# GpSimd jobs one step later, and a running account of GpSimd's load, in an attention and MoE kernel

## The chip, the cores and the metric

The kernel runs on one core of a Trainium2 chip, in one launch. The metric is the device time of that launch in microseconds (us), as a median over several runs. The engines are TensorE (PE, with its weight loads PEld), VectorE (DVE), ScalarE (ACT), GpSimd (POOL) and SyncE (SP). Each works through its own instructions in the order of the program and waits for others by semaphores.

## The reference

Attention over B = 8 batches, H = 8 heads, S = 576 positions, D = 64, in float32, where each row keeps its 32 highest scores; then a mixture of experts with one expert of eight per token. Cut to what matters:

```python
scores = scale * np.matmul(q, k.transpose(0, 1, 3, 2))      # 8 x 8 x 576 x 576
kth = np.partition(scores, -32, axis=-1)[..., -32:-31]
attn = softmax of the scores that are >= kth                # the others are masked
x = matmul(attn, v), transposed to (8 * 576, 512)           # 4608 tokens
logits = x @ w_gate                                         # 8 experts
expert, gate_w = argmax(logits), its softmax probability
out[token] = gate_w * (relu(x @ w1[expert]) @ w2[expert])   # 512 -> 1024 -> 512
```

## The kernel before, in words

**The attention loop.** A loop over steps t takes 16 half batches n of NT = 9 steps s each, 144 steps in all. A step handles two tiles of 128 rows. PE computes their scores three steps ahead and ACT copies them to SBUF (tile sb). VectorE finds the 32nd highest score of each row: 21 MAX8 over parts of sb into cand (L1025), then rounds of MAX8 and MATCH_REPLACE8 on cand that fill vq (L1033). GpSimd makes the bound nb from vq (L1007), ACT the sign of sb against nb (sg, L454), and GpSimd adds sg to sb in two instructions (L455), "the pair". This pair marks what is masked. PE then transposes sb (tt, L461), ACT takes exponentials, and PE multiplies by the values (px, L477 and L492).

**Side jobs.** Everything else is cut into generators, each in one of the lanes prep0, prep1, sums, rows, redo, patch, find, route. Once a step, `advance` goes through the lanes by due time and lets each run to its next `yield`. A `need(...)` states what the next piece takes of each engine; a piece whose need would bring what was spent in this step above `LIMITS` waits for a later step, as does one whose s is not among its `at`. `need(slack=1)` is a pause of a step without a price; after the loop, where no limits hold, it is skipped. What a piece does on PE, ACT, VectorE and GpSimd goes to queues that are flushed at fixed places of the step; VectorE's pieces are interleaved with the rounds of the search. The scatters of `route` and the DMAs on SP's queue are emitted at once.

The jobs that matter here, once for each batch b:

- sums: ACT writes exponentials of the kept values over vq, GpSimd adds them up (vq 128x288 down to 128x18, and tiny), VectorE takes the reciprocal (rinv). apart, cnt and wild on GpSimd count what was kept.
- find: rows for which the search may have kept a wrong number are looked for and up to 128 of them are picked: r_key, r_ok, r_sl, r_qx on VectorE, a product with r_qx on PE (r_li), then r_fl on VectorE, and gathers by r_fl of r_at and r_nb and by r_at of the scores r_sb, on GpSimd.
- redo: does these rows again: r_wk and r_v on VectorE, then a subtraction r_sb by r_wk on GpSimd, exponentials r_et, the product of rv and r_et on PE (L265), and r_xa. patch writes them over the first result (scatters lps, xs). Their pieces may run at the steps s in FREE, FREE2 and FREE3 only.
- rows: normalises the output (xm, lp, xl, lpl on VectorE) and stores it as tokens xs.
- route: gate logits lg, expert choice oh, hist and cum on VectorE, positions po and pos, the payload pay, and five scatters into `table` on GpSimd, each with a spacer ahead (L846 and L847). Batch 4 fixes the rows of the first expert, batch 5 those of four more (`ahead`): for these two all five scatters go out in one piece, followed by hist x ones on PE, skip and ebase on VectorE and the loads of the indices ids.

top, a running maximum over the half batches, is updated by GpSimd at the last step of each.

**The MoE part.** After the loop the remaining jobs are drained, first on their own until the first expert is routed, then piece by piece with the steps of the generator `moe`. It goes through units (an expert and up to some tiles of 128 tokens); each has eight steps f over F = 1024. A step is a hidden product H (ph, L1159), and the projection of the step before (y, L1174). Its weights are split in a high and a low part: wh on ACT or VectorE, wl on VectorE for w1 and on GpSimd for w2 (L957). Unit 0's weights are split ahead, into the tiles rv and kt. Rows of a unit are gathered by GpSimd (kt for unit 0 and gx later, L876), turned by PE (mt and ph from kt or gx, L1139) and split by ACT (xh) and VectorE (xl). From f = 3 on, the tiles of the next unit are turned one a step, if they have been gathered by then; if not, all are turned together ahead of that unit's first step. A unit's rows can be gathered only when route has run for the batch that fixes them.

L265 is the line of a helper that flushes the queues, so most jobs stand under it.

Of the kernel before, what the change touches and what calls it, by code (L numbers as in the profile page):

```python
# [14 lines left out]
OP = mybir.AluOpType  # L15
# [22 lines left out]
CAP = 640  # L38
TAIL = 1
TADV = 5  # L40
FREE = (1, 2, 3, 4, 5)
FREE2 = (1, 2, 3, 4)
FREE3 = (1, 2, 3)
DUE = dict(redo=4, patch=12, sums=0, rows=0, find=3, route=12)
LIMITS = dict(pool=3.5, act=1.6, dve=2.0, pe=3.0)


@with_exitstack
def attention_moe(ctx, tc, q, k, v, w_gate, w1, w2, out):
    nc = tc.nc  # L50
# [37 lines left out]
    NT = 2 * MAIN + 1  # L88
# [98 lines left out]
    top = consts.tile([128, 1], F32, name="top")  # L187
# [76 lines left out]
    def later(queue):  # L264
        return lambda f, *a, **k: queue.append(lambda: f(*a, **k))  # L265

    pe, act, vec, pool = later(pq), later(aq), later(dq), later(gq)
# [8 lines left out]
    def need(**k):  # L276
        return k
# [157 lines left out]
    MX = {}  # L435
# [178 lines left out]
    def j_find(b):  # L614
# [39 lines left out]
        yield need(dve=0.1)  # L654
        fl = sm("r_fl", [128, 1], I32)
        vec(nc.vector.scalar_tensor_tensor, fl, li[:, 1:2], float(NLT + 1), li[:, 0:1], op0=OP.mult, op1=OP.add)
        yield need(pool=2.0)
        at = sm("r_at", [128, 4], I32)
        pool(nc.gpsimd.indirect_dma_start, out=at, out_offset=None, in_=atab,
# [129 lines left out]
    def j_route(b):  # L789
# [49 lines left out]
        vec(nc.vector.tensor_reduce, sm, ex, axis=AX.X, op=OP.add)  # L839
        vec(nc.vector.tensor_scalar, sm, sm, 1e-9, None, op0=OP.add)  # L840
        vec(nc.vector.reciprocal, pay[:, :, 2].bitcast(F32), sm)
        for c in range(KB):
            if c == 0 or b not in ahead:
                yield need(pool=1.0)
            n = 128 if c < MAIN else LEFT
            nc.gpsimd.memset(spacer, 0.0)  # L846
            st = nc.gpsimd.indirect_dma_start(  # L847
                out=table, out_offset=bass.IndirectOffsetOnAxis(ap=pos[0:n, c:c + 1], axis=0),
                in_=pay[0:n, c, :], in_offset=None)
            for o in scat:  # L850
                tc.declare_no_dep(st.ins, o.ins, reason="each token has a slot of its own")
            scat.append(st)
# [30 lines left out]
    ROUTED = set()  # L883
    lanes = {k: [] for k in ("prep0", "prep1", "sums", "rows", "redo", "patch", "find", "route")}
    wants = {}

    def start(lane, job, due=0):
        lanes[lane].append((due, job))
# [1 line left out]
            wants[lane] = next(job)  # L890

    def advance(limits=LIMITS, s=None):
        spent = {}
        for name in sorted((k for k in lanes if lanes[k]), key=lambda k: lanes[k][0][0]):
            lane, want = lanes[name], wants[name] or {}
            want = dict(want)
            if s not in want.pop("at", (s,)) and s is not None:
                continue
            want["bank"] = want.get("bank", 0) + want.pop("spot", 0)
            if not att_open[0]:  # L900
                want["bank"] += want.pop("nook", 0)
            if want.get("bank", 0) > len(free) or want.get("nook", 0) > cell[0]:
                continue
            if limits and any(spent.get(r) and spent[r] + want[r] > limits[r] for r in want if r in limits):
                continue
            for r in want:
                spent[r] = spent.get(r, 0.0) + want[r]
            cell[0] -= want.get("nook", 0)
            wants[name] = next(lane[0][1], lanes)
            while not limits and wants[name] and wants[name] is not lanes and wants[name].get("slack"):  # L910
                wants[name] = next(lane[0][1], lanes)
            if wants[name] is lanes:
                wants[name] = None
                lane.pop(0)
                if lane:
                    wants[name] = next(lane[0][1])

    def drain(more=None):
        while any(lanes.values()):
# [84 lines left out]
    for t in range(steps + LAG + TD + 4):  # L1004
        n, s = divmod(t, NT)
        if delayed:
            delayed[0](*delayed[1])  # L1007
        if grp(t - LAG - TD - 1):
            exps(t - LAG - TD - 1)
        if grp(t - LAG):  # L1010
            softmax(t - LAG, grp(t - LAG), 0)
        scores(grp(t + LA))
        if grp(t - LAG):
            softmax(t - LAG, grp(t - LAG), 1)
        if grp(t - LAG - TD - 2):
            av(t - LAG - TD - 2, grp(t - LAG - TD - 2))
        scores_left(grp(t + LA))
        if grp(t - LAG - TD):
            transp(t - LAG - TD)
        flush(pq)  # L1020
        flush(aq)
        one, two, last = topk(t, grp(t)) if grp(t) else ([], [], None)
        for m in range(max(len(one), 1)):
            if m < len(one):
                one[m][0](*one[m][1])  # L1025
        delayed = last
        if t == 1:
            settle(first_pt, [0, 1, 2, 3], lambda: release(first_pt))
            mine_, dq[:] = dq[:], []
            flush(mine_)  # L1030
        mine, dq[:] = dq[:], []
        for m, (f, a) in enumerate(two):
            f(*a)  # L1033
            if mine and m >= 2:
                mine.pop(0)()
        flush(mine)
        if t == 0:
            nc.vector.tensor_reduce(top, VQ[0][:, 0:2, 0], axis=AX.X, op=OP.max)
            first_pt = bank()
            spread(first_pt)  # L1040
            pq.pop()()
        if s == NT - 1 and n in MX:
            pool(nc.gpsimd.tensor_scalar, top, MX.pop(n), top, None, op0=OP.max)
        m = t - LAG + 1
        if m > 0 and m % (2 * NT) == 0:
            start("find", j_find(m // (2 * NT) - 1), t + DUE['find'])
            start("redo", j_redo(m // (2 * NT) - 1), t + DUE['redo'])
        m = t - LAG
        if 0 <= m < steps and m % NT == NT - 1:
            start("sums", j_sums(m // NT), t + DUE['sums'])  # L1050
            if m == steps - 1 and len(lanes["sums"]) == 1:

                for _ in range(2):
                    wants["sums"] = next(lanes["sums"][0][1])
                flush(gq)
                flush(aq)
        if t < steps:
            advance(s=s)
            flush(gq)
        else:  # L1060
            for _ in range(TAIL if t < steps + TADV else 0):
                advance(None)
                for queue in (gq, pq, aq, dq):
                    flush(queue)
        for at, job, a in AHEAD if first else ():
            if t - steps == at:
                job(*a)
        m = t - LAG - TD - 3
        if m >= 0 and m % NT == NT - 1:
            start("rows", j_rows(m // NT), t + DUE['rows'])  # L1070
        if s == PA:
            prep(2 * n + 4)
        if s == PB:
            prep(2 * n + 3)
        if s == LQ and n + 2 < NQ:
            load_qk(n + 2)
        if s == LV and 0 < n < NQ:
            load_v(n)
# [367 lines left out]
    n = over(moe_a, counts, cap, otab, lambda: next(g))  # L1446
# [50 lines left out]
```

## Time and profile before

| | |
|---|---|
| runs | 1308.88, 1307.54, 1308.72 us; median 1308.72 |
| profiled execution | 1306.47 us, its span 1304.6 us, granted clock 0.984 |
| busy, share of the span | PE 1217.7 us (93%), PEld 968.0 (74%), DVE 1019.4 (78%), ACT 828.3 (63%), POOL 833.6 (64%) |
| chain of waits, share | DVE 51%, PE 36%, POOL 4%, issue 4%, DMA 2%, ACT 2%, SP's queue 1% |

The attention loop ends with VectorE's last search at 762.4 us. The first matmul of the MoE part (mt from kt) starts at 787.97 us. The chain lies on VectorE in the loop and on PE in the MoE part; the shares over the whole span mix the two. A row of the timeline gives start and duration in us, engine, line, operation, and in brackets the engine's idle time before it with what ended it.

### The profile page before, as it was taken

What the parts mean: (1) busy time and instruction counts of PE and PEld (TensorE: products, weight loads), DVE (VectorE), ACT (ScalarE), POOL (GpSimd) and SP (SyncE); (2) the same over time, 40 slices, a digit from 0 to 9 for tenths busy, and PEclk for the clock granted to TensorE, in tenths of its full rate; (3) what the DMA queues carried; (4) which work ended last, traced back from release to release, by engine and by line L of the source; (5) the groups of instructions that cost most, each with busy time, mean ns of one, the idle gap of its engine ahead of it and who ended that gap; (6) DMA issues with size and microseconds to landing.
All of it is one profiled execution on the core that took longest, in us unless ns stands there. A gap on an engine that the chain in (4) does not pass through costs nothing.

```text
span 1304.6 us, 31672 instructions
## 1 busy us (share of the span) xinstructions
PE 1217.7 (93%) x9126; PEld 968.0 (74%) x9126; DVE 1019.4 (78%) x6889; ACT 828.3 (63%) x1691; POOL 833.6 (64%) x1205
## 2 busy tenths in 40 slices
PE   6999999999999999999998878999899999999997
PEld 3667666776666666667676667888899989889996
DVE  7998999999999999999998965645773333345664
ACT  4999789898888888887996843333332323233432
POOL 4676766877867867868867866675554324155654
PEclk9999999999999999999998988999999999999999
DMA  6755565655655655555553615645564434256774
GB/s 168 228 176 180 174 188 157 185 172 159 190 164 156 194 178 170 167 173 168 182 174 110 191 39 163 189 118 170 138 184 139 121 99 127 79 157 191 223 212 125
DMA packets 271239, 211.18 MB, mean 162 GB/s; under 512 B 136216, under 2 KB 214216, under 8 KB 271056
## 3 DMA queue, kind: packets, MB, share of 16 engines
q1 hardware_dynamic: 260320, 185.92, 48.2%
q0 software_dynamic: 9504, 22.86, 5.4%
q8 instruction: 74, 1.21, 0.4%
q14 instruction: 109, 0.89, 0.2%
q10 hardware_dynamic: 1232, 0.30, 0.1%
HBM read 102.49 MB, written 107.90 MB: 161 GB/s over the span
## 4 chain that ended last, share of the span: by engine, by line
DVE 51%; PE 36%; POOL 4%; issue 4%; DMA 2%; ACT 2%; SPq 1%; POOLq 0%; DVEq 0%; ACTq 0%
DVE cand L1025 25%; PE ph L1159 16%; PE y L1174 16%; DVE cand L1033 10%; DVE vq L1033 9%; PE mt L1139 1%; DVE xm L265 1%; PE pt L265 1%; POOL sb L455 1%; POOL table L847 1%; DMA gx<-xs,ids 1%; DVE r_v L265 1%; DVE r_qx L265 1%; POOL wl L957 1%; SPq L113 1%
## 5 line engine op out<-in xcount | busy, mean ns | idle before, releaser
L455 POOL TENSOR_TENSOR sb<-sb,sg 128x576 f32<-128x576 f32 x288 | 370.0, 1301 | 50.7 <-ACT sg L454 41.1
L1025 DVE MAX8 cand<-sb 128x8 f32<-128x52 f32 (+2 forms) x3024 | 368.5, 208 | 0.2 <-issue 0.2
L957 POOL TENSOR_TENSOR wl<-r,wh 128x512 fp32r<-128x512 f32 x110 | 142.0, 1292 | 223.4 <-DVE wh L956 219.0
L454 ACT ACTIVATE sg<-sb,nb 128x576 int8<-128x576 f32 x288 | 228.9, 795 | 60.8 <-POOL sb L455 60.8
L477 PEld LDWEIGHTS px<-et,rv 128*64 128x64 f32 x2688 | 130.2, 137 | 122.0 <-ACT xt L265 49.0
L1160 ACT ACTIVATE hh<-ph 128x320 fp32r<-128x320 f32 (+3 forms) x136 | 58.2, 428 | 241.2 <-PE ph L1159 214.5
L1033 DVE MAX8 vq<-cand 128x8 f32<-128x22 f32 (+7 forms) x1152 | 200.6, 205 | 0.0
L461 PE MATMUL tt<-turner,sb 128*128 128x128 f32 x1296 | 177.7, 279 | 22.2 <-POOL sb L455 18.7
L367 PE MATMUL ps<-qk 64*128 64x512 f32 (+1 forms) x576 | 185.7, 653 | 4.2 <-ACT sb L369 3.5
L1161 DVE SCALAR_TENSOR_TENSOR hl<-ph,hh 128x320 fp32r<-128x320 f32 (+3 forms) x136 | 65.1, 479 | 150.3 <-ACT hh L1160 124.1
L467 ACT ACTIVATE et<-tt,shift 128x1152 f32<-128x1152 f32 x144 | 178.2, 1237 | 2.5 <-PE tt L461 2.5
L477 PE MATMUL px<-et,rv 128*64 128x128 f32 (+1 forms) x2688 | 163.5, 267 | 13.4 <-ACT xt L265 8.0
L461 PEld LDWEIGHTS tt<-turner,sb 128*128 128x128 f32 x1296 | 147.9, 144 | 34.4 <-POOL sb L455 29.3
L1159 PE MATMUL ph<-xh,wh 128*128 128x320 f32 (+3 forms) x536 | 168.2, 314 | 0.0
L1159 PE MATMUL ph<-xh,wl 128*128 128x320 f32 (+3 forms) x536 | 164.8, 307 | 0.0
L1159 PE MATMUL ph<-xl,wh 128*128 128x320 f32 (+3 forms) x536 | 164.6, 307 | 0.0
L1033 DVE MATCH_REPLACE8 cand<-vq,cand 128x22 f32<-128x22 f32 (+2 forms) x864 | 158.6, 189 | 0.0
L369 ACT ACTIVATE sb<-ps 128x1024 f32<-128x1024 f32 x144 | 149.0, 1034 | 10.3 <-PE ps L367 10.3
L1174 PE MATMUL y<-wh,hl 128*128 128x512 f32 x324 | 128.4, 396 | 0.0
L1174 PE MATMUL y<-wh,hh 128*128 128x512 f32 x324 | 127.7, 394 | 0.5 <-ACT yo L1178 0.5
L1174 PE MATMUL y<-wl,hh 128*128 128x512 f32 x324 | 127.9, 395 | 0.0
L1159 PEld LDWEIGHTS ph<-xh,wh 128*128 128x128 f32 x536 | 101.0, 188 | 3.9 <-issue 1.0
(261 smaller groups left out, 2174.4 us busy)
## 6 DMA issues: line engine op xcount, KB each, us to landing
r<-in_moe_w_dram SPq DMA_DIRECT2D x220, 256.0 KB
sc<-sb SPq DMA_DIRECT2D x128, 288.0 KB
sc<-sb SPq DMA_DIRECT2D x128, 256.0 KB
rv<-in_v_dram SPq DMA_DIRECT2D x32, 256.0 KB
xs<-xm SPq DMA_DIRECT2D x16, 512.0 KB
rq<-in_q_dram SPq DMA_DIRECT2D x60, 128.0 KB
rk<-in_k_dram SPq DMA_DIRECT2D x60, 128.0 KB
sc<-sb SPq DMA_DIRECT2D x32, 144.0 KB
```

What stands on the lines that cost most here:

```text
L367: nc.tensor.matmul(MAINS[:, n], qk[:, 0, w], qk[:, 1, 2 * LEFT:], start=True, stop=True)
L369: nc.scalar.activation(bass.AP(EX[-1].tensor, EX[-1].offset, [list(EX[-1].ap[0]), [S + LEFT, 2], [1, M]]), MAINS, AF.Copy)
L454: nc.scalar.activation(upper(SG[i]), SB[u], AF.Sign, bias=nb[:, i, 1:2], accum_out=CNT[b][:, 2 * lt + i:2 * lt + i + 1])
L455: nc.gpsimd.tensor_tensor(SB[u], SB[u], SG[i], op=OP.add)
L461: nc.tensor.matmul(tt[:, c], x[:, c * 128:(c + 1) * 128], ident, start=True, stop=True, is_transpose=True)
L467: nc.scalar.activation(ET[t], three.rearrange("p (c q) -> p c q", c=NB9), AF.Exp, bias=shift[:, t // NT, 0:1], scale=0.125)
L477: yield lambda kb=kb, blk=blk: nc.tensor.matmul(px[h * 64:(h + 1) * 64], block(rv, p % 2, kb if kb < MAIN else MAIN + n, h), et[:, blk, q] ...
L957: (nc.gpsimd if i else nc.vector).tensor_tensor(lo, r, hi, op=OP.subtract)
L1025: one[m][0](*one[m][1])
L1033: f(*a)
L1159: nc.tensor.matmul(ph, a[:, c, :], x[:, c, s], start=(m == 0), stop=(m == len(seq) - 1))
L1174: nc.tensor.matmul(PY[u, t], a[:, s], x, start=(f == 0 and m == 0), stop=(f == FC - 1 and m == 2))
```

## The change

Three things change in the order in which jobs are handed out:

- FREE, FREE2, FREE3 move by one step; find pauses a step between r_fl and its gathers, route one between pay and the first scatter; top is updated at the first step of the next half batch instead of the last of its own.
- The pool limit of a step falls from 3.5 to 3.0.
- What a step has spent on GpSimd above ROOM = 2.2 is carried into the next as `debt` and counts there as spent.

```diff
-FREE = (1, 2, 3, 4, 5)
-FREE2 = (1, 2, 3, 4)
-FREE3 = (1, 2, 3)
+FREE = (2, 3, 4, 5, 6)
+FREE2 = (2, 3, 4, 5)
+FREE3 = (2, 3, 4)
-LIMITS = dict(pool=3.5, act=1.6, dve=2.0, pe=3.0)
+ROOM = 2.2
+LIMITS = dict(pool=3.0, act=1.6, dve=2.0, pe=3.0)
...
         vec(nc.vector.scalar_tensor_tensor, fl, li[:, 1:2], float(NLT + 1), li[:, 0:1], op0=OP.mult, op1=OP.add)
+        yield need(slack=1)
         yield need(pool=2.0)
...
         vec(nc.vector.reciprocal, pay[:, :, 2].bitcast(F32), sm)
+        yield need(slack=1)
         for c in range(KB):
...
+    debt = [0.0]
...
     def advance(limits=LIMITS, s=None):
-        spent = {}
+        spent = {"pool": debt[0]} if limits and debt[0] else {}
...
+        if limits:
+            debt[0] = max(spent.get("pool", 0.0) - ROOM, 0.0)
...
-        if s == NT - 1 and n in MX:
-            pool(nc.gpsimd.tensor_scalar, top, MX.pop(n), top, None, op0=OP.max)
+        if s == 0 and n - 1 in MX:
+            pool(nc.gpsimd.tensor_scalar, top, MX.pop(n - 1), top, None, op0=OP.max)
```

Lines of the changed kernel are numbered a little higher: L1007 becomes L1014, L847 L850, L876 L879, L957 L964, L1139 L1146.

In the loop, GpSimd's order around the gathers of batch 2, before. nb and two sb rows are the work of a step; r_at and r_nb are the gathers by r_fl:

```order
L455 TENSOR_TENSOR sb<-sb,sg_145 128x576
L846 MEMSET spacer 1x1
L847 DMA table<-pay,pos 36864x4
L265 TENSOR_SCALAR top<-mx_n,top 128x1
L265 DMA r_at<-atab,r_fl 128x4
L265 DMA r_nb<-ntab_5133,r_fl 128x2
L1007 TENSOR_TENSOR nb_232<-vq,factors 128x4
L455 TENSOR_TENSOR sb<-sb,sg_143 128x576
```

and with the change:

```order
L456 TENSOR_TENSOR sb<-sb,sg_143 128x576
L456 TENSOR_TENSOR sb<-sb,sg_145 128x576
L266 TENSOR_SCALAR top<-mx_n,top 128x1
L266 IOTA pay 128x5
L1014 TENSOR_TENSOR nb_232<-vq,factors 128x4
L456 TENSOR_TENSOR sb<-sb,sg_143 128x576
L456 TENSOR_TENSOR sb<-sb,sg_145 128x576
L266 DMA r_at<-atab,r_fl 128x4
L266 DMA r_nb<-ntab_5098,r_fl 128x2
L266 TENSOR_SCALAR apart<-vq,shift 128x18
L266 TENSOR_TENSOR cnt<-cnt,apart 128x18
L266 TENSOR_SCALAR apart<-vq,shift 128x18
```

top now comes after the pair of the next step and the gathers a step later, together with the counts apart, cnt and wild.

Between the loop and the MoE part, GpSimd's order before, from the second kt gather to the first of the four additions that finish the sums of the last half batch:

```order
L876 DMA kt<-xs,ids_12353 128x512
L846 MEMSET spacer 1x1
L847 DMA table<-pay,pos 36864x4
L846 MEMSET spacer 1x1
L847 DMA table<-pay,pos 36864x4
L846 MEMSET spacer 1x1
L847 DMA table<-pay,pos 36864x4
L846 MEMSET spacer 1x1
L847 DMA table<-pay,pos 36864x4
L846 MEMSET spacer 1x1
L847 DMA table<-pay,pos 36864x4
L265 TENSOR_TENSOR vq<-vq 128x18x8
```

and with the change, from the same gather on:

```order
L879 DMA kt<-xs,ids_13110 128x512
L266 TENSOR_TENSOR vq<-vq 128x18x8
L266 TENSOR_TENSOR vq<-vq 128x18x4
L266 TENSOR_TENSOR vq<-vq 128x18x2
L266 TENSOR_TENSOR vq<-vq 128x18
L266 TENSOR_TENSOR vq<-vq,tiny 128x18
L964 TENSOR_TENSOR rv_13422<-rq,rv_13421 128x512
L964 TENSOR_TENSOR kt<-rk,kt 128x512
L266 IOTA pay 128x5
L964 TENSOR_TENSOR wl_13568<-r_13525,wh_13567 128x512
L849 MEMSET spacer 1x1
L850 DMA table<-pay,pos 36864x4
```

The five scatters of batch 5 stood ahead of the sums and now stand behind the first wl of the MoE part.

The gathers of unit 1 on GpSimd before, where wl is the second of the MoE part:

```order
L957 TENSOR_TENSOR wl_13629<-r_13592,wh_13628 128x512
L875 MEMSET spacer 1x1
L876 DMA gx<-xs,ids_13517 128x512
L875 MEMSET spacer 1x1
L876 DMA gx<-xs,ids_13517 128x512
L875 MEMSET spacer 1x1
L876 DMA gx<-xs,ids_13517 128x512
L265 DMA r_at<-atab,r_fl 128x4
```

and with the change, where the last wl ahead of them is the sixth:

```order
L964 TENSOR_TENSOR wl_13760<-r_13704,wh_13759 128x512
L266 TENSOR_TENSOR r_xa<-r_xa 128x256
L266 TENSOR_TENSOR r_xa<-r_xa 128x128
L266 TENSOR_TENSOR r_xa<-r_xa 128x64
L964 TENSOR_TENSOR wl_13819<-r_13754,wh_13818 128x512
L878 MEMSET spacer 1x1
L879 DMA gx<-xs,ids_13784 128x512
L878 MEMSET spacer 1x1
L879 DMA gx<-xs,ids_13784 128x512
L878 MEMSET spacer 1x1
L879 DMA gx<-xs,ids_13784 128x512
```

They come four wl later, behind the scatters and the pieces of find and redo of the last batches. Since they come later, PE's order changes as well. Before, four transposes of gx at a time stood between the steps of unit 0:

```order
L1174 MATMUL y_13638<-wh_13597,hh 128x512
L1174 MATMUL y_13638<-wl_13598,hh 128x512
L1174 MATMUL y_13638<-wh_13597,hl 128x512
L1139 MATMUL mt<-turner,gx 128x128 x4
L265 MATMUL pt_247<-turner,xt 128x144 x2
L265 MATMUL pt_247<-turner,xt 64x144 x2
```

and with the change all twelve stand behind unit 0, ahead of the first hidden product of unit 1 (ph 128x384):

```order
L1181 MATMUL y_13618<-wh_13759,hh 128x512
L1181 MATMUL y_13618<-wl_13760,hh 128x512
L1181 MATMUL y_13618<-wh_13759,hl 128x512
L1146 MATMUL mt<-turner,gx 128x128 x12
L1166 MATMUL ph<-xh,wh_13874 128x384
L1166 MATMUL ph<-xl_13945,wh_13874 128x384
L1166 MATMUL ph<-xh,wl_13875 128x384
```

The rv x r_et products of batch 6, ten matmuls each, move too: both stood ahead of the r_qx product in the gap, now one stands between it and the first mt, and one behind the first projection of unit 0.

## The prediction

> **What bounds the kernel now.** I read the busy time of three stretches first: the attention loop up to VectorE's last top-k search, the gap up to the first MoE matmul, and the MoE part.
>
> ```profile
> 0.00:762.50 762.50, 701.23 (x6135) 505.80 (x6136) 744.30 (x6346) 647.74 (x1329) 552.86 (x875) 0.99 0.57 171
> 762.50:788.00 25.50, 16.57 (x129) 13.16 (x128) 10.87 (x32) 9.01 (x17) 20.49 (x34) 0.80 0.24 61
> 788.00:1304.60 516.60, 499.93 (x2868) 449.05 (x2864) 264.22 (x512) 171.59 (x345) 260.26 (x297) 0.99 0.51 153
> ```
>
> The columns after the length are PE, PEld, DVE, ACT, POOL. VectorE (DVE) is busy 744.30 of 762.50 us in the loop, so an edit is worth there what it takes from VectorE's own queue. In the 25.5 us of the gap POOL leads with 20.49. In the MoE part PE is busy 499.93 of 516.60. Three places, three owners: an edit to GpSimd's order counts where GpSimd makes the owner wait, or where the owner's instruction runs longer beside GpSimd's.
>
> A loop step without side jobs, the last two steps, and the end of the last:
>
> ```profile
> 745.05 1.14 DVE L1025 MAX8 cand<-sb 128x8 f32<-128x52 f32 x9
> 749.63 1.02 DVE L1025 MAX8 cand<-sb 128x8 f32<-128x52 f32 x8
> 756.14 1.02 DVE L1025 MAX8 cand<-sb 128x8 f32<-128x52 f32 x8
> 762.39 0.53 DVE L265 TENSOR_TENSOR xm<-pt,rinv 128x384 f32<-128x384 f32 x1
> ```
>
> Each row is the first search of a step (the last: what follows the final one). The bare step is 749.63 - 745.05 = 4.58; steps 142 and 143 take 6.51 and 6.25, the excess being side jobs interleaved with the search.
>
> **The loop, part by part.** Excess that is not work but waiting shows in three side jobs and one wait:
>
> ```profile
> L265 DVE SCALAR_TENSOR_TENSOR r_fl<-r_li x8: 148/783/1428, 143.8 to 798.3; 128x1 int32<-128x1 f32 x8
> L265 DVE TENSOR_TENSOR r_wk<-sg,r_sb x8: 745/750/1779, 182.4 to 818.1; 128x576 f32<-128x576 bf16 x8
> L265 DVE TENSOR_TENSOR hist<-oh,valid x8: 321/792/1210, 287.8 to 893.1; 128x40 bf16<-128x40 f32 x8
> DVE skip L265 <- PE pt L265: 5.5, 1, 5.5
> 327.64 2.52 POOL L455 TENSOR_TENSOR sb<-sb,sg 128x576 f32<-128x576 f32 x2
> 328.76 1.43 DVE L265 SCALAR_TENSOR_TENSOR r_fl<-r_li 128x1 int32<-128x1 f32 x1
> ```
>
> The last two rows give the mechanism: r_fl has one element per partition, and beside GpSimd's pair of mask additions (327.64 to 330.16) it ends at 330.19, when the pair does. Here POOL was late, so its pair lay over r_fl; where POOL is on time r_fl takes 0.148.
>
> (1) r_fl. Four of the eight are long (the median, 783, is halfway between 148 and some 1,420). The change puts top, r_at and r_nb a step behind what they read; POOL no longer waits for VectorE in its queue ahead of the pair, and r_fl's step has an early pair. -4 x 1.28 = -5.1 us (ends: 0 and -5.1).
> (2) r_wk and hist. Two r_wk (at 182.4 and 369.0) are 1.0 longer than the median, and four hist in the loop take the median, 0.47 over the shortest: -2.0 and -1.9; the new steps of hist have a short queue on POOL. Ends: 0 and -3.9.
> (3) r_wk's new place. It moves from steps 70, 88, ... to 72, 90, 108, 126, right after POOL's heaviest stretch. The prices on POOL:
>
> ```profile
> 326.48 0.98 POOL L847 DMA_INDIRECT table<-pay,pos  x1 [0.16 <-issue]
> 345.73 0.20 POOL L1007 TENSOR_TENSOR nb<-vq,factors 128x4 f32<-128x4 f32 x1
> 345.88 2.52 POOL L455 TENSOR_TENSOR sb<-sb,sg 128x576 f32<-128x576 f32 x2
> 348.79 1.65 POOL L265 TENSOR_TENSOR r_xa<-r_xa 128x256 f32<-128x256 f32 x3
> 357.78 1.53 POOL L265 TENSOR_TENSOR vq<-vq 128x144 f32<-128x144 f32 x4
> ```
>
> nb and the pair are 2.67 a step, an indirect DMA with its spacer 1.26. In the new order POOL has, in the eight steps before r_wk's, 8 x 2.67 = 21.4; nine indirect DMAs = 11.3; r_xa 1.65; sums 1.8; about 4.8 of small operations: 41.0. VectorE's eight steps are 8 x 4.58 and 2.8 of jobs = 39.4. So POOL comes to that step about 1.6 us late, and the pair ends 1.6 us into r_wk, which comes 2.84 into a step. Four times: +6.4 (ends: 0 where POOL is on time, and 4 x 2.5, the whole pair, = +10.0). I take 1.6 because the sum gives it. [...]
>
> (4) Work leaves the loop. The r_wk group of batch 6 (step 142: 6.51 - 4.58 - 0.28 for rinv, as at 784.17 below, = 1.6) and the lg group of batch 5 (step 143: 6.25 - 4.58 - 0.53 for xm = 1.1) come after the last search, where VectorE waits for POOL anyway: -2.7. If that cover were gone, 0.
> (5) The skip wait. Its chain:
>
> ```profile
> 690.27 1.09 POOL L847 DMA_INDIRECT table<-pay,pos  x1 [2.42 <-DVE vq L1033]
> 698.52 2.51 POOL L455 TENSOR_TENSOR sb<-sb,sg 128x576 f32<-128x576 f32 x2
> 709.52 0.16 DVE L265 TENSOR_SCALAR skip<-pt 128x1 f32<-128x1 f32 x1 [5.50 <-PE pt L265]
> ```
>
> Batch 4's five scatters go in one burst; the next pair starts at 698.52, PE's transposes wait for it, hist x ones stands behind them on PE, and skip behind that on VectorE. In the new order the burst still stands in one piece, but without the 2.42, and skip comes four steps after it instead of three. I take 5.5 down to 2.3 (0.3 to 1.9 more recovered by one more step): -3.2, ends 0 and -5.5.
>
> Loop: -5.1 - 3.9 + 6.4 - 2.7 - 3.2 = -8.5.
>
> **The gap before MoE.**
>
> ```profile
> 775.74 0.09 POOL L846 MEMSET spacer<- 1x1 f32 x1
> 782.30 1.53 POOL L265 TENSOR_TENSOR vq<-vq 128x144 f32<-128x144 f32 x4
> 784.17 0.28 DVE L265 RECIPROCAL rinv<-vq 128x8 f32<-128x8 f32 x2 [5.24 <-POOL vq L265]
> 787.72 0.37 PE L265 MATMUL pt<-rhs,r_qx 128*128 128x2 bf16 x8 [4.59 <-DVE r_qx L265]
> 787.97 1.09 PE L1139 MATMUL mt<-turner,kt 128*128 128x128 f32 x4
> 775.29 2.60 PE L265 MATMUL pt<-rv,r_et 128*128 128x256 f32 x10
> ```
>
> Batch 5's five scatters fill POOL from 775.74 to 782.30, and the last sums, rinv, r_qx and the first MoE transposes (mt) wait in a row for that. The change puts these scatters behind the sums: -6.6. The r_sb subtraction now ahead of the sums costs 0.4 (the rest falls in a POOL wait), and the first of the two rv x r_et products, which lay under the scatters, now stands between r_qx and mt: +2.5. Together -3.7; ends -6.2 (the product finds cover) and -1.5 (VectorE is late with batch 5's lg group).
>
> **The MoE part.** The second rv x r_et product moves from the gap to unit 0: +2.5, since PE is full there. The larger term is unit 1's rows:
>
> ```profile
> 786.53 2.03 POOL L265 TENSOR_TENSOR r_xa<-r_xa,r_hm 128x512 f32<-128x512 f32 x1
> 796.19 1.29 POOL L957 TENSOR_TENSOR wl<-r,wh 128x512 fp32r<-128x512 f32 x1 [7.63 <-DVE wh L956]
> 799.92 1.02 POOL L876 DMA_INDIRECT gx<-xs,ids  x1 [0.16 <-issue]
> 802.81 0.95 POOL L876 DMA_INDIRECT gx<-xs,ids  x1 [0.22 <-issue]
> 804.79 0.60 PE L1139 MATMUL mt<-turner,gx 128*128 128x128 f32 x4
> 806.06 0.69 DVE L1141 TENSOR_TENSOR xl<-mt,xh 128x512 fp32r<-128x512 f32 x1 [0.50 <-ACT xh L1140]
> 814.72 2.55 POOL L957 TENSOR_TENSOR wl<-r,wh 128x512 fp32r<-128x512 f32 x2
> 819.55 0.33 PE L1159 MATMUL ph<-xh,wh 128*128 128x384 f32 x1
> 876.31 5.26 DMA gx<-xs,ids
> 791.71 0.63 PE L1159 MATMUL ph<-xh,rv 128*128 128x256 f32 x2
> 794.91 0.49 PE L1159 MATMUL ph<-xh,rv 128*128 128x256 f32 x2
> ```
>
> Times from mt (787.97). Now the gathers go out at +12 and the three tiles are turned between steps of unit 0; unit 1's first matmul is at 819.55, +31.6. In the new order the five scatters follow the first wl on POOL, and the gathers follow the sixth, so that all twelve transposes stand together in front of unit 1. First wl at +8.2; from there to the end of the sixth wl POOL takes 21.1 now, of which 4.1 are gathers and 1.0 a wait; with 6.6 of scatters and 2.0 of r_xa,r_hm it is 24.6. Gathers at +33.0; a gather that PE waited for took 5.26 to its use: first tile +38.3, third 2.6 later, and mt to the end of xl 2.0: unit 1 starts at +42.9, against +34.1 with the product alone. That is +8.8; with 1.0 for r_xa,r_hm (as it runs undisturbed) 7.8: I take +8.3. Ends: +3.7, if rows land with the issue's end, and +9.
>
> After such a pause PE may run slow: after the 4.59 above, two matmuls took 0.63 at 791.71 and not before 794.91 less, half speed for 4.3, some 2.1 lost. I take +1.5, between 0 and 2.1. [...]
>
> MoE: 2.5 + 8.3 + 1.5 = +12.3. Order and waits after unit 1 stay, as PE paces them.
>
> **Sum**: -8.5 - 3.7 + 12.3 = +0.1 on the profiled 1306.47. The median of the runs is 1308.72, 0.2% above it, so 1308.8: no measurable change (0.2%, 2.6 us, is about what can be told).
>
> **Rivals.**
> A, faster: r_wk is not behind the pair, since POOL arrives on time (1.6 us in 41 is small, and jobs of the loop are spread by the account). The +6.4 goes: 1302.4. For it: six of eight r_wk take 0.75 now. Against: the 41.0 against 39.4.
> B, faster: unit 1's rows land early. At the low end (+3.7, clock kept) MoE costs 6.2: 1302.7. For it: the first gather of 799.92 was used at 804.79 without a wait. Against: the third gather's issue alone ends near +37.
> C, slower: POOL falls further behind in unit 0. Its list there is 24.6 us without a hole, and r_xa,r_hm takes 2.03 beside VectorE; every us later starts unit 1 a us later. From 2.5 it decides; at 4, wl is late for PE too: 1313. Against: each wl waits for a cast of VectorE that follows PE, so the list cannot fall behind by much more than its own length.
> D: nothing moves, since VectorE was 98% busy and GpSimd only followed: 1308.7. Against: r_fl, and the 5.5 at skip.
>
> **How the numbers follow.** As summed: 0.42, of which 0.29 falls within 0.2%, 0.06 below and 0.07 above. A 0.21, B 0.10, C 0.22, D 0.05. Faster 0.06 + 0.31 = 0.37, same 0.29 + 0.05 = 0.34, slower 0.07 + 0.22 = 0.29. The range reaches beyond A and C, whose other terms vary by a few us: 1300.5 to 1315.5; my own case alone has 1304 to 1313.
>
> **What the profile will show.** Right: r_fl at 0.15 in all loop steps; r_wk near 2.3 in four; POOL waits for mx_n gone; a skip wait of 1 to 3.5; the gap at 21 to 22.5; a PE wait of 5 to 6 for gx ahead of unit 1. Wrong: r_wk at 0.75 (A), a gx wait of 2 (B) or 9 (C), or PE waiting for wl in unit 0.

## The result, and the profile after

| | before | after |
|---|---|---|
| median of the runs, us | 1308.13 (1305.07 to 1308.88) | 1321.21 (1318.64 to 1322.18) |
| span of the profiled execution, us | 1304.6 | 1316.9 |
| granted clock | 0.984 | 0.978 |

The change makes the kernel slower: the ratio is 1.0102, with a 95% interval of 1.0085 to 1.0119. The forecast was no change, 1308.8 us, with 1315.5 as the upper end. The profiled run of the changed kernel is the fastest of its four, so its stages add up to 12.3 more than before where the medians differ by 13.1.

The same three stretches of the changed kernel (length, then PE, PEld, DVE, ACT, POOL busy; the first value behind them is the granted clock):

```profile
0.00:758.03 758.03, 698.22 (x6125) 505.00 (x6127) 740.84 (x6332) 650.23 (x1325) 547.61 (x874) 0.99 0.59 172
758.03:783.42 25.39, 16.40 (x130) 12.97 (x129) 16.36 (x46) 10.15 (x21) 16.06 (x24) 0.82 0.37 104
783.42:1316.90 533.48, 508.60 (x2875) 455.81 (x2874) 268.05 (x512) 172.16 (x345) 266.18 (x307) 0.97 0.49 146
```

The loop is 4.4 us shorter (758.03 against 762.47), where 8.5 was forecast. The gap is 25.4 as before, where 3.7 less was forecast. The MoE part is 16.8 longer, where 12.3 was forecast. All three miss in the same direction, so that 0.1 became 12.3.

**The loop.** The side jobs of VectorE in the changed kernel (count, then min/median/max in ns), and two of them before:

```profile
L266 DVE SCALAR_TENSOR_TENSOR r_fl<-r_li x8: 144/160/455, 143.5 to 793.8; 128x1 int32<-128x1 f32 x8
L266 DVE TENSOR_TENSOR hist<-oh,valid x8: 316/325/371, 307.6 to 905.8; 128x40 bf16<-128x40 f32 x8
L266 DVE TENSOR_TENSOR r_wk<-sg,r_sb x8: 737/1212/1857, 186.9 to 815.7; 128x576 f32<-128x576 bf16 x8
L266 DVE SCALAR_TENSOR_TENSOR r_key<-cnt,idx x8: 185/742/774, 110.1 to 767.6; 128x36 f32<-128x36 f32 x8
L266 DVE COPY hist<-cum x8: 177/623/1066, 308.4 to 906.7; 128x8 bf16<-128x8 bf16 x8
```

```profile
L265 DVE SCALAR_TENSOR_TENSOR r_key<-cnt,idx x8: 183/186/196, 110.1 to 770.3; 128x36 f32<-128x36 f32 x8
L265 DVE COPY hist<-cum x8: 173/177/561, 289.1 to 894.0; 128x8 bf16<-128x8 bf16 x8
```

r_fl and hist are short everywhere, as forecast. r_wk is long in four steps, by 1.0 each. Two operations that the forecast never looked at are new on the list: r_key rose from 0.19 to 0.74 in five steps, and the copy into hist from 0.18 to 1.06 in four. How they come to wait (GpSimd's pair and VectorE's operation, at three places):

```profile
386.51 2.52 POOL L456 TENSOR_TENSOR sb<-sb,sg 128x576 f32<-128x576 f32 x2
388.32 0.76 DVE L266 SCALAR_TENSOR_TENSOR r_key<-cnt,idx 128x36 f32<-128x36 f32 x1
...
403.29 2.52 POOL L456 TENSOR_TENSOR sb<-sb,sg 128x576 f32<-128x576 f32 x2
403.55 1.07 DVE L266 COPY hist<-cum 128x8 bf16<-128x8 bf16 x1
...
375.08 2.51 POOL L456 TENSOR_TENSOR sb<-sb,sg 128x576 f32<-128x576 f32 x2
376.44 1.78 DVE L266 TENSOR_TENSOR r_wk<-sg,r_sb 128x576 f32<-128x576 bf16 x1
```

An addition of the pair is half of 2.52. r_key starts in the second one and ends with it (389.08 against 389.03). The copy starts in the first and ends with the first (404.62 against 404.55). r_wk starts just behind the first (376.44 against 376.34) and ends 0.63 behind the second (378.22 against 377.59). So each waits for the one addition that runs when it comes. Before, the wait also went the other way: eight of the 288 additions ran long, 1.53 to 2.33, four of them begun while r_wk ran. In the changed kernel none takes over 1.30, so of the two it is VectorE alone that waits there.

**The skip wait** went from 5.5 to 4.5. The burst has moved, but more work stands behind it:

```profile
738.18 0.91 POOL L850 DMA_INDIRECT table<-pay,pos  x1 [0.22 <-issue]
739.11 1.53 POOL L266 TENSOR_TENSOR vq<-vq 128x144 f32<-128x144 f32 x4
743.52 1.66 POOL L266 TENSOR_TENSOR r_xa<-r_xa 128x256 f32<-128x256 f32 x3
751.09 0.16 DVE L266 TENSOR_SCALAR skip<-pt 128x1 f32<-128x1 f32 x1 [4.55 <-PE pt L266]
```

The last scatter is followed by the end of a sum and by r_xa, 3.2 in all, before GpSimd catches up with the pairs that PE needs ahead of hist x ones.

**The gap.** ScalarE, GpSimd and PE between the last search (758.03) and the first MoE matmul:

```profile
761.67 0.78 ACT L266 ACTIVATE r_wk<-r_sb,r_nb 128x576 bf16<-128x576 f32 x1 [4.39 <-DVE r_v L266]
762.35 1.20 ACT L468 ACTIVATE et<-tt,shift 128x1152 f32<-128x1152 f32 x1
764.39 2.51 POOL L456 TENSOR_TENSOR sb<-sb,sg 128x576 f32<-128x576 f32 x2 [3.19 <-ACT sg L455]
777.24 2.25 DVE L266 TENSOR_TENSOR r_qx<-slots,r_sl 128x1024 bf16<-128x1024 bf16 x1
779.76 3.73 PE L266 MATMUL pt<-rv,r_et 128*128 128x256 f32 x10
783.42 1.12 PE L1146 MATMUL mt<-turner,kt 128*128 128x128 f32 x4
```

The redo of batch 6 now comes after the last search. ScalarE's part of it waits 4.39 for r_v and stands in ScalarE's queue ahead of the last exponentials (et) and signs (sg); GpSimd's last pair waits for these, and the sums, r_qx and mt follow it.

**The MoE part**, from GpSimd's first wl to unit 1's first product; the last three rows are of the chain of waits:

```profile
791.75 1.29 POOL L964 TENSOR_TENSOR wl<-r,wh 128x512 fp32r<-128x512 f32 x1 [13.24 <-PE ph L1166]
798.62 0.91 POOL L850 DMA_INDIRECT table<-pay,pos  x1 [0.22 <-issue]
815.64 1.05 POOL L879 DMA_INDIRECT gx<-xs,ids  x1
820.81 0.66 PE L1146 MATMUL mt<-turner,gx 128*128 128x128 f32 x4 [4.14 <-DMA gx<-xs,ids]
822.88 1.11 PE L1146 MATMUL mt<-turner,gx 128*128 128x128 f32 x4 [1.41 <-DVE xl L1148]
825.40 1.12 PE L1146 MATMUL mt<-turner,gx 128*128 128x128 f32 x4 [1.41 <-DVE xl L1148]
827.21 0.69 PE L1166 MATMUL ph<-xh,wh 128*128 128x384 f32 x1 [0.69 <-ACT xh L1147]
828.42 0.52 PE L1166 MATMUL ph<-xh,wl 128*128 128x384 f32 x1
...
815.64 5.12 DMA gx<-xs,ids
885.74 6.86 DMA gx<-xs,ids
893.82 3.62 PE ph L1166 x12
```

Unit 1 starts 43.8 after the first MoE matmul (827.21 - 783.42), against 31.6 before: +12.2. Its first product runs at half clock (0.52 a matmul, where 0.33 is usual) and costs 2.3, of which 1.7 remain from the third step on. The granted clock was 0.50 in it, and 1.00 in that of the kernel before. The gather of unit 3's rows took 6.86 to its use, against 5.26 before: PE waits 4.85 for them (3.48 before), and the product behind this wait starts 1.7 later still. It is slow too, 3.62 for 12 matmuls at a granted clock of 0.55, another 1.6. These are the 16.8 within 0.4.

### The profile page after: what moved, and what is told of

The parts are those of the page before. It is cut to its first block, busy times and chain, and to the rows that moved or that the text cites. A ratio compares the mean times of both kernels' runs of the same rounds, so it can differ in the third digit from the quotient of the medians.

```text
span 1316.9 us, 31664 instructions
## 1 busy us (share of the span) xinstructions
PE 1223.2 (93%) x9126; PEld 973.8 (74%) x9126; DVE 1025.2 (78%) x6889; ACT 832.5 (63%) x1691; POOL 829.9 (63%) x1205
## 4 chain that ended last, share of the span: by engine, by line
PE 43%; DVE 34%; POOL 7%; issue 5%; ACT 5%; DMA 4%; SPq 2%; POOLq 0%; DVEq 0%; ACTq 0%
DVE cand L1032 16%; PE ph L1166 16%; PE y L1181 15%; DVE cand L1040 7%; DVE vq L1040 6%; PE pt L266 3%; POOL sb L456 3%; PE ps L368 2%; PE px L478 2%; PE mt L1146 2%; ACT sg L455 2%; PE tt L462 1%; DMA gx<-xs,ids 1%; ACT sb L370 1%; DMA rv<-in_v_dram 1%
## 5 line engine op out<-in xcount | busy, mean ns | idle before, releaser
L456 POOL TENSOR_TENSOR sb<-sb,sg 128x576 f32<-128x576 f32 x288 | 363.6, 1280 | 42.9 <-ACT sg L455 34.2
L964 POOL TENSOR_TENSOR wl<-r,wh 128x512 fp32r<-128x512 f32 x110 | 142.6, 1297 | 233.5 <-DVE wh L963 216.9
L455 ACT ACTIVATE sg<-sb,nb 128x576 int8<-128x576 f32 x288 | 225.7, 784 | 24.5 <-POOL sb L456 24.2
L478 PEld LDWEIGHTS px<-et,rv 128*64 128x64 f32 x2688 | 132.0, 139 | 118.0 <-ACT xt L266 47.4
L1014 POOL TENSOR_TENSOR nb<-vq,factors 128x4 f32<-128x4 f32 x144 | 29.1, 202 | 142.7 <-DVE vq L1040 108.2
```

What stands on the lines that cost most here:

```text
L455: nc.scalar.activation(upper(SG[i]), SB[u], AF.Sign, bias=nb[:, i, 1:2], accum_out=CNT[b][:, 2 * lt + i:2 * lt + i + 1])
L456: nc.gpsimd.tensor_tensor(SB[u], SB[u], SG[i], op=OP.add)
L478: yield lambda kb=kb, blk=blk: nc.tensor.matmul(px[h * 64:(h + 1) * 64], block(rv, p % 2, kb if kb < MAIN else MAIN + n, h), et[:, blk, q] ...
L964: (nc.gpsimd if i else nc.vector).tensor_tensor(lo, r, hi, op=OP.subtract)
```

## The experiments

All by stage: the ratio to before with its interval, the end of VectorE's last search, the gap from there to the first MoE matmul, from there to unit 1's first matmul, and from that to the end of the last engine instruction, behind which every span goes on for about 6.5 (us, one profile each; two profiles of one order differ by up to 2 in a stage).

| run | ratio | search ends | gap | to unit 1 | rest |
|---|---|---|---|---|---|
| before | | 762.5 | 25.5 | 31.6 | 478.5 |
| after | 1.0102 (1.0085 to 1.0119) | 758.0 | 25.4 | 43.8 | 483.1 |
| e1_free_shift | 0.9982 (0.9971 to 0.9993) | 758.3 | 21.2 | 34.4 | 482.0 |
| e2_no_find_pause_last | 0.9989 (0.9973 to 1.0005) | 760.7 | 24.4 | 30.8 | 482.9 |
| e3_top_and_route_pause | 0.9936 (0.9919 to 0.9953) | 753.4 | 25.4 | 32.4 | 479.6 |
| e4_find_pause_and_shift | 1.0146 (1.0118 to 1.0173) | 770.6 | 24.4 | 38.5 | 485.9 |
| e5_without_find_pause | 0.9961 (0.9945 to 0.9977) | 752.1 | 20.6 | 34.8 | 483.6 |
| e6_exp_first | 1.0079 (1.0062 to 1.0097) | 758.6 | 20.5 | 47.4 | 483.2 |
| e7_turn_in_three_banks | 1.0061 (1.0038 to 1.0084) | 757.4 | 24.3 | 40.2 | 484.0 |
| e8_no_idle_before_unit_1 | 1.0094 (1.0076 to 1.0111) | 758.8 | 24.3 | 43.6 | 483.7 |
| e9_route_sooner | 1.0101 (1.0075 to 1.0127) | 757.0 | 25.9 | 47.0 | 479.1 |
| e10_no_find_pause_route_sooner | 0.9879 (0.9857 to 0.9900) | 749.8 | 20.5 | 39.7 | 471.9 |
| e11_route_pause_alone | 0.9957 (0.9938 to 0.9977) | 754.2 | 25.4 | 32.4 | 479.1 |
| e12_top_alone | 0.9979 (0.9964 to 0.9995) | 759.0 | 25.7 | 31.2 | 480.9 |
| e13_no_idle_at_all | 1.0053 (1.0031 to 1.0074) | 757.5 | 24.3 | 41.8 | 482.0 |
| e14_r_key_and_r_wk_later | 1.0073 (1.0049 to 1.0097) | 755.5 | 26.5 | 45.6 | 484.5 |
| e15_best_with_r_wk_later | 0.9947 (0.9927 to 0.9968) | 759.6 | 21.7 | 43.4 | 471.9 |

### Which part of the change costs

**e1**, before with `FREE`, `FREE2`, `FREE3` shifted alone:

> The kernel before with FREE, FREE2 and FREE3 moved by one step and nothing else of the change. Theory A (a late tail: a shift of one step puts batch 5's route so late that unit 1's rows are gathered after unit 0's sixth wl, and all twelve transposes stand together ahead of unit 1): unit 1 starts with its three tiles turned one after the other, but the scatters already ran in the gap, so the rows have landed; the chain of three tiles costs some 5 us against 1.3 now, and PE runs at half clock behind it (1 to 2): 1312 to 1315. Rival B (the loss comes from GpSimd's work in the loop, by the account and the lower limit): no change, 1308.

A miss: it is a little faster. The order in unit 1 is the one with all twelve transposes together, but here the gathers go out 46 after the last search and not 58, so unit 1 loses only 2.8, and 3.5 later; loop and gap win 8.5.

**e2**, the changed kernel with find's pause for the first six batches only:

```diff
-        yield need(slack=1)
+        if b < 6:
+            yield need(slack=1)
```

> The changed kernel, with find's pause left out for batches 6 and 7 only; the loop up to step 135 is the same as in the changed kernel. In its order unit 1's tiles are turned between the steps of unit 0 again, both rv x r_et products stand ahead of the gap's end, and skip stands four steps after the burst, in step 140. Theory A: the 16.8 us of the MoE part go away, and the gap shrinks by the scatters: 1301 to 1306. Rival B: the loss stays with the loop's order: 1318 to 1322.

The loss at unit 1 is gone (30.8), and with it the whole of the slowdown: batch 5's first scatter goes out 19 after the last search and unit 1's first gather 36, against 35 and 58 in the changed kernel. 4.4 stay in the rest, most of it in waits for later units' rows. The total is at the upper end of A.

**e3**, before with top a step later and route's pause, **e11** with route's pause alone, **e12** with top alone:

> The kernel before with only two parts of the change: top one step later, and route's pause. The tail is that of the kernel before; skip stands in step 136, six steps after the burst instead of three. Theory A: the skip wait (5.5 us) goes, and with POOL no longer waiting for mx_n ahead of a pair, the long r_fl shrink (up to 5 us): 1298 to 1304. Rival C (a wait taken from POOL comes back somewhere else in the loop, since VectorE was busy nearly all the time): 1306 to 1309.

> Before, with route's pause alone. A (its pay no longer keeps GpSimd waiting, and skip comes six steps behind the burst of scatters): the skip wait falls from 5.5 to under 1, r_fl stays long in four steps: 1301 to 1304. B (the pause helps only once GpSimd's waits for the running maximum are gone): skip 3 or more, 1305 to 1308.

> Before, with top a step later alone. A (GpSimd's wait for mx_n in its queue is what makes the pair late where r_fl comes): r_fl 0.15 in all steps, skip still 5.5: 1301 to 1304. B (the waits for pay make it late): r_fl long in four steps, 1306 to 1308.

e3 is as expected, and faster than both kernels. Apart, the two parts do other things than I thought. r_fl in e11, then in e12, and the skip wait in the same order:

```profile
L265 DVE SCALAR_TENSOR_TENSOR r_fl<-r_li x8: 147/150/657, 141.4 to 790.1; 128x1 int32<-128x1 f32 x8
L265 DVE SCALAR_TENSOR_TENSOR r_fl<-r_li x8: 148/439/1421, 143.4 to 795.0; 128x1 int32<-128x1 f32 x8
...
DVE skip L265 <- PE pt L265: 1.1, 2, 0.6
DVE skip L265 <- PE pt L265: 5.5, 2, 5.0
...
POOL table L847 <- DVE vq L1033: 12.0, 5, 2.4
```

Route's pause alone shortens r_fl and the skip wait; with top alone r_fl stays long in four steps and skip waits 5.0. The last row shows GpSimd waiting for VectorE ahead of a scatter, in e12 as before; in e11 these five waits are gone. So what made the pair late for r_fl was a scatter that waited for pay in GpSimd's queue, not the running maximum. hist does the opposite: it stays at 0.8 in e11 and is 0.32 in e12.

**e4**, before with find's pause and the shift of `FREE`:

> The kernel before with find's pause and the FREE shift alone (the pause cannot stand without the shift), without the account, route's pause and top. Theory A: this carries the whole loss of the tail: 1316 to 1322. Rival B: without the account the loss is gone: 1306 to 1310.

Slower than expected: the loop alone loses 8.1. GpSimd is late there because it waits in its queue, and VectorE then waits for it:

```profile
DVE skip L265 <- PE pt L265: 7.5, 1, 7.5
DVE r_key L265 <- POOL cnt L265: 3.1, 3, 1.7
DVE mm L265 <- ACT stat L265: 1.5, 1, 1.5
```

So the other parts of the change (route's pause, top, the account) take back some of what find's pause costs; which of them does it in the loop I did not separate.

**e5**, the changed kernel without find's pause:

```diff
         vec(nc.vector.scalar_tensor_tensor, fl, li[:, 1:2], ...)
-        yield need(slack=1)
         yield need(pool=2.0)
```

> The changed kernel without the pause of find; all other parts are in. A (the pause of find brings r_wk behind the pair, the new waits of r_key and of the copies into hist, and batch 5's late routing): the loop as in the run with top and route alone (-9), the gap as in the run with the shift of FREE alone (-4), the MoE part +3 to +7: 1298 to 1304. B (the account of GpSimd's load spreads jobs so that VectorE's short operations meet the pair): the loop near -3, so 1305 to 1310.

As expected, though the MoE part is 8.3 longer than before and not 3 to 7. It is 1.4% faster than with the pause: the loop wins 5.9, the gap 4.8 and unit 1's start 9.0. In this kernel r_key is 0.19 in the loop steps and the copy into hist 0.17, and batch 5's first scatter goes out 18 after the last search, against 35 with find's pause and 14 before. Adding the pause to the shift of `FREE` costs the like (e1 to e4, 1.6%). This one line is the slowdown. It is not what lengthens r_wk: in the steps of the loop r_wk stands 3.5 over its shortest in all, against 4.0 with the pause, and 3.7 in e3.

### What the three stages lose

**e6**, the changed kernel with ScalarE's r_wk of batch 6 one round later:

```diff
+        if b == B - 2:
+            for _ in range(1):
+                yield
         yield need(act=0.6)
```

> The changed kernel, with ScalarE's r_wk of batch 6 one round later in the drained part, so that the last et and sg stand ahead of it. A (ScalarE's queue held back the last pair of GpSimd and with it the sums and r_qx: 4.39 us at r_wk): the last pair starts at least 2.5 earlier, the gap falls from 25.4 to 21 to 23; one product of r_et moves into the MoE part (+2.5 there): 1317 to 1319.5. B (the gap is set by another chain, GpSimd's own list or the late products): gap 25, 1321 to 1323.

```profile
759.32 4.99 POOL L456 TENSOR_TENSOR sb<-sb,sg 128x576 f32<-128x576 f32 x4
```

The two last pairs now stand back to back, the second from 761.8, 3.2 after the last search and not 6.4, and r_qx comes 2.4 sooner. The gap is 4.9 shorter, 2.4 of it by that and 2.5 because the product with r_et moves behind mt. A holds for the gap. But unit 1 starts 67.9 after the last search, against 69.2: its gathers went out only 1.1 earlier, and 3.6 of the 4.9 come back there. The two ratios, 1.0079 and 1.0102, have intervals that meet, so that the stages show more here than the whole.

**e7**, tiles 2 and 3 of unit 1 turned in the banks of ph:

```diff
-        pt = ps_a.tile([128, DC, 128], F32, name="mt") if u or not t else \
+        pt = ps_a.tile([128, DC, 128], F32, name="mt") if u > 1 or not t else \
```

> The changed kernel, with tiles 2 and 3 of unit 1 turned in the two banks of ph instead of the one of mt. A (the single bank makes the three tiles serial: two waits of 1.41 for xl): unit 1 starts 2.0 to 2.8 earlier, 1318 to 1319.5. B (the third gather's landing sets the start): 0 to 1 earlier, 1320 to 1321.

From the first tile to the first product it is 3.6 (818.31 to 821.87), against 6.4: the 2 x 1.41 are gone. The median fell by more than that and lies below the range of A. Part of the rest is not the edit's: in the profiles of e7, e8 and e13, whose order is that of the changed kernel up to unit 1's tiles, PE had its full clock at the end of the gap (granted 1.00; the product with r_et 2.60, unit 0's first product 3.83), and in the changed kernel's it had not (0.67 and 0.55; 3.73 and 5.68). Executions of one order differ there.

**e8** and **e13**, extra matmuls ahead of unit 1's tiles (`wp` is a bank of ph):

```diff
...
+                    for m in range((14, 4, 4)[t]):            # e13: (44, 9, 9)
+                        nc.tensor.matmul(wp, W[k][0][:, 0, :], XP[0][0][:, 0, 0:256], ...)
                     turn_x(u, t)
```

> The changed kernel with 14, 4 and 4 extra matmuls of 256 columns ahead of the three tiles of unit 1, on data that is there, their result unused. A (PE runs at half speed in unit 1's first hidden product because it idled 4.1 and 2 x 1.4 us before): that product takes 4.4 instead of 6.6, unit 1's second step starts about 2 earlier, 1318.5 to 1319.5. B (it is slow for another reason, such as operands that arrive late): no change or the extra work is lost, 1321 to 1323.

> The changed kernel with 44, 9 and 9 extra matmuls of 256 columns ahead of the three tiles of unit 1 (5.3, 1.1 and 1.1 us at full clock), so that PE hardly idles there; their result is unused. A (the idle 4.1 us sets the clock back): the first hidden product of unit 1 runs at 0.33 a matmul and not 0.52 to 0.69, and the second step of unit 1 starts 1.5 to 2.3 earlier, less what the extra matmuls delay: 1317 to 1319. B (another cause): 0.52 and more remains, 1319 to 1322.

e8 alone decided nothing: the 14 ran at once and PE still idled 4.46 behind them. It serves as the comparison for e13, since gap and unit 0 ran at the same clock in both. In e13 PE idled 0.5, and the clock held:

```profile
812.22 5.43 PE L1228 MATMUL ph<-xh,wh 128*128 128x256 f32 x44
818.16 0.66 PE L1146 MATMUL mt<-turner,gx 128*128 128x128 f32 x4 [0.51 <-DMA gx<-xs,ids]
824.83 0.34 PE L1166 MATMUL ph<-xh,wh 128*128 128x384 f32 x1
```

Tiles turn in 0.66 each and matmuls take 0.34, where e8 has 1.12 and 0.52; the granted clock in unit 1's first product is 1.00, against 0.50. Unit 1's second step starts 3.6 earlier than in e8 by its distance from the first MoE matmul: 1.7 ahead of the first product and 1.9 behind its start. The ratios, 1.0053 and 1.0094, have intervals that do not meet, and e13 lies below the range of A. Extra work that makes the kernel faster shows that the idle time had set the clock back: unit 1's first product had a granted clock of 0.50 behind the 4.14 idle in the changed kernel and the 4.46 in e8, and 1.00 behind the 0.51 in e13. Ahead of unit 3's rows PE idled 3.48 in the kernel before, with 1.00 in the product behind it, and 4.85 in the changed kernel, with 0.55.

**e9**, the changed kernel with one more round of the side jobs ahead of each MoE step until batch 5 is routed, and **e10**, the same without find's pause:

```diff
             if more is not None:
+                for _ in range(1 if max(b for b, _ in part_of) not in ROUTED else 0):
+                    for queue in (pq, aq, dq):
+                        flush(queue)
+                    advance(None)
+                    flush(gq)
                 next(more)
```

> The changed kernel, where the drained side jobs get one more round ahead of each MoE step until batch 5 is routed: its scatters are followed by two wl less on GpSimd until the gathers of unit 1, and the three tiles are turned one a step. A (unit 1's late rows are the loss in the MoE part, with the slow PE after the pause): unit 1 starts 33 to 37 after the first MoE matmul instead of 43.8, no PE wait for gx ahead of it, 1306 to 1312. B (GpSimd's list of small jobs sets it, in whatever order): 41 to 44, 1317 to 1321.

> The changed kernel without the pause of find, and with that extra round. A (the savings add): loop -10, gap -5 against before, unit 1 after 31 to 33 instead of 34.8, the rest 1 to 3 less than without the extra round: 1292 to 1297. B (what is saved ahead of unit 1 comes back as later waits for unit 2's rows): 1299 to 1302.

e9 missed: gathers 53 after the last search instead of 58, but the tiles now stand earlier in PE's queue, which waits 9.5 for the first. What the edit spares comes back as that wait. e10 went further than A, to 1290.28 us, 1.2% faster than before and the fastest of all, but not by all the terms of A: loop and gap win what was expected or more, unit 1 starts after 39.7 and not 31 to 33, since the extra rounds stand ahead of it, and the rest is 11.7 shorter than in e5 and not 1 to 3. There batch 5's scatters are early (18 after the last search), the gathers come at 42, and the whole MoE part to the end takes 511.6, against 526.9 after and 510.1 before, while loop and gap keep their 17.6. Its three stretches:

```profile
0.00:749.85 749.85, 698.81 (x6139) 503.51 (x6141) 738.44 (x6340) 651.10 (x1329) 548.31 (x875) 0.99 0.59 174
749.85:770.36 20.51, 15.76 (x127) 12.31 (x124) 14.48 (x38) 8.71 (x17) 16.23 (x27) 0.83 0.32 91
770.36:1288.50 518.14, 498.95 (x2870) 448.90 (x2866) 261.66 (x512) 171.30 (x346) 264.29 (x304) 0.99 0.52 152
```

**e14**, the changed kernel with r_key and r_wk nine instructions of the search later in their step, and **e15**, e10 with r_wk so:

```diff
+        dq.extend([lambda: None] * 9)
         vec(nc.vector.tensor_tensor, wk, SGR, sb, op=OP.subtract)
```

> The changed kernel with r_key and r_wk nine instructions of the search later within the same step; nothing else moves. A (both wait for the addition that GpSimd runs at that moment): r_key 0.19 and r_wk 0.75, the loop 5 to 7 shorter, 1312 to 1315. B (VectorE waits at whatever comes beside the pair): the waits show up at r_v or at the search, 1317 to 1321.

> The kernel without find's pause and with the extra round for route, and r_wk nine instructions later. A: its excess of 3.1 goes, 1287 to 1288.5. B (the group behind r_wk ends later than the search and what waits for it is late): 1290 to 1292.

B, mostly. In e14 r_key and r_wk are short, 6.8 less in all, but the last operation on r_v now meets the pair of the next step:

```profile
L266 DVE SCALAR_TENSOR_TENSOR r_v<-r_v x8: 167/964/970, 189.6 to 816.0; 128x8 f32<-128x8 f32 x8
380.76 2.51 POOL L456 TENSOR_TENSOR sb<-sb,sg 128x576 f32<-128x576 f32 x2
381.10 0.96 DVE L266 SCALAR_TENSOR_TENSOR r_v<-r_v 128x8 f32<-128x8 f32 x1
```

It ends with the first addition (382.06 against 382.02); six of these cost 4.9, and the loop is 2.6 shorter instead of 5 to 7. e15 lost to e10, 0.9947 against 0.9879, and lies outside both of its ranges. Its loop took 9.8 longer, of it 4.0 in VectorE's busy time, where r_v meets the pair as in e14; of the rest, 1.9 and 1.8 stand in steps 132 and 142 and 2.3 in step 1, which the edit does not touch. Why so much, stays open.

## Why the prediction was wrong

The sum failed in all three stages, each time by what it left out: in the loop r_key and the copy into hist (6.4 together), in the gap ScalarE's queue (2.5), in the MoE part the wait for unit 3's rows and the slow product behind it (3.3).

**Right.** That the loop wins and the MoE part loses; r_fl (-4.7, forecast -5.1); that r_wk meets the pair in four steps; the place and start of unit 1: first wl at +8.3 (forecast +8.2), gathers at +32.2 (+33.0), unit 1 at +43.8 (+42.9), and half clock after the wait (1.7 lost, forecast 1.5). The wait for gx is 4.1 for 5 to 6, with two waits of 1.41 for the bank behind it.

**Step (1) named the wrong releaser.** r_fl is short because of route's pause (e11), not because of top (e12), so the size came out right with the wrong wait. GpSimd's waits for mx_n ahead of top (27.0 in the loop before) did go, but in e12 they go as well and r_fl stays long. In step (2) hist came out as forecast, but its new steps are not needed for that: top alone, in the old steps, does it (e12).

**Step (3)** is the term r_wk: +6.4 forecast, +4.0 measured (1.0 each). GpSimd's pair ends 1.0 to 1.2 into r_wk, not 1.6. Nor is the new place the reason that the forecast took it for: in e3 and e5 r_wk stands in its old steps and is about as long. What brings it there is open; the kernels with route's pause and top together have 3.1 (e10) to 4.0, either alone has 1.6 (e11) or 1.9 (e12), and before has 2.0. The forecast's upper end let r_wk wait for the whole pair (4 x 2.5), as the r_fl row does. The r_key, copy, r_wk and r_v rows show a wait for one addition, the one that ran when they came: r_key ends 0.05 behind it in its five long steps, the copy into hist, 128x8, 0.04 behind it in four, r_v 0.04 in e14's row, and r_wk, which takes 0.75 undisturbed, 0.62 to 0.63 behind it. r_fl had come 0.15 to 0.17 before the end of the first addition, and the second followed without a hole.

**The failing step of the loop is what its sum left out.** It followed the operations that were long before, and not those that become long: five r_key (+2.8) and four copies into hist (+3.6). Without find's pause both are short (e5). These, the skip wait (-1.0 instead of -3.2, since a sum and r_xa stand behind the burst) and r_fl (0.4) are 9.0 worse than forecast; r_wk is 2.4 better, hist as forecast. That makes 6.6 where the loop fell short by 4.1; the 2.5 between I did not trace.

**The gap** (-3.7 forecast, -0.1 measured). The scatters did leave: r_qx comes 19.2 after the last search, against 22.9. The miss is 2.5 there, which is ScalarE's queue (2.4 by e6), and the product with r_et, which took 3.73 on a slow PE instead of 2.5; since the same order has 2.60 in e7, e8 and e13, this part belongs to the one execution and not to the change. I had moved batch 6's redo out of the loop at no cost ("where VectorE waits for POOL anyway"), and named no queue that it stands in ahead of others: that cover was VectorE's, and the cost lay on ScalarE.

**The MoE part** (+12.3 forecast, +16.8 measured). Unit 1's start was sized within 1.4 (+12.2 where the rows and the product made 10.8). "Order and waits after unit 1 stay, as PE paces them" failed: the gather for unit 3 cost 3.3 more. The slow PE at the start of unit 0, which the forecast read as 4.3, lasts 7.0 in the kernel before (granted 0.50 from 788 to 795), but it is in both kernels and so not in the difference.

**Rival C**, 1313, had the sign, by another mechanism: GpSimd did not fall behind in unit 0; its list there took what the forecast gave it. And gap and MoE part are not two terms: GpSimd's list runs from the last search to the gathers, so 3.6 of the 4.9 won in e6's gap came back in unit 1.

## What to carry to other kernels

When jobs are shifted by a step, list every operation of the other engine that will stand beside the instruction it has to wait for (here GpSimd's additions), not only those that stand there now. Follow the last job of a chain of deferred jobs to the next stage: here one pause put a table's scatters 17 us later, and with them the rows that PE waits for. A deferred piece that "falls into a wait" has to be checked on each engine it touches: here ScalarE waited 4.39 for it, and the last et and sg stood behind it in the queue.

## What the runs showed of the hardware

A VectorE copy of eight bf16 elements per partition took 0.18 alone and 1.06 beside GpSimd's addition (changed kernel), and an addition begun while r_wk ran took up to 1.89 where 1.28 is usual (before): each of the two engines was in some places the one that waited. r_fl, which came 0.15 to 0.17 before the end of an addition with the next right behind, got no turn between the two and took 1.41 to 1.43 (before). Three tiles that PE turned through one PSUM bank cost two waits of 1.41 in the changed kernel, which are gone with three banks (e7). And 62 matmuls whose result nobody reads made the kernel faster, 1.0053 against 1.0094 with 22 of them that left PE idle for 4.46: with the 62, PE idled 0.51 there and its granted clock in the product behind was 1.00, against 0.50 (e13, e8).
